# A decode block on one Trainium2 core: the Down loads in two pieces, the end products in two PSUM banks

## The chip, the cores and the metric

The kernel runs on one core of a Trainium2 chip. The metric is the time of one execution in microseconds, as the device reports it. Before the change it was 263.92 us (median of 3 runs, 263.78 to 263.95). Lower is better.

## The reference

One decode step of a transformer block in float32, for 8 sequences with one new token each and a width of 1024: attention over the last 1024 positions of a cache (32 query heads, 4 key and value heads of 128), then a gated MLP with an inner width of 3584. Cut to what matters:

```python
x = A_x                                                   # 8 x 1 x 1024
h = x + attention(layernorm(x))                           # wq, caches, softmax, wo
g = layernorm(h) @ w_gate                                 # 1024 x 3584
u = layernorm(h) @ w_up                                   # 1024 x 3584
h2 = h + (gelu_tanh(g) * u) @ w_down                      # 3584 x 1024: "Down"
```

With only 8 rows of activations the arithmetic is small. What has to be moved is 111 MB of weights and caches.

## The kernel before, in words

All weights and caches come as one stream of loads into two halves of a large SBUF tile `w`, `wbuf[0]` ("a") and `wbuf[1]` ("b"), of 8 MB each. Twelve units of 8 MB fill the two in turn: two for each of wq, K, V, wo, Gate and Up in sets of columns. Every load is issued by SP, in program order, on one queue; a load waits until TensorE has done with the half that it overwrites (`half_a`, `half_b`: marks on TensorE's semaphore).

TensorE runs a loop (L230) over 8 turns. A turn has a product over half b, `half(1, ...)`, then a fold of its four partial sums (L236, `y_sb` and `add2`), then 8 transposes of `source` (L241), then a product over half a, `half(0, ...)`; the turns in `NO_B` and `NO_A` leave one of them out. A product is 8 steps c = 0 to 7, each with 4 matmuls side by side in four column strips of the array (L223); a matmul of 512 columns in float32 gives two records in the trace, so one step has 8 records and one product 64. Waits inside a product come from the list of gates given to `half`: at c = 0 the load's semaphore (`go[0]` or `go[1]`), at later steps `go_later`, where a number of 1 stands for one step of another engine and of 16 for one load. As the loop is the same code for every turn, GpSimd sets `go_later` ahead of time for all turns but the last (L196).

The MLP's last matrix, Down, is 3584 x 1024: 28 chunks of 128 rows, each 0.5 MB. Eight of them (`EARLY`) ride in the units of Gate and Up. The next 16 (`HEAD`) go into `wbuf[0]`, two chunks for each step c, in loads of 10, 4 and 2 chunks (`PARTS`; names `wd0` to `wd2`, tensor `dn`), all released by the end of the product over the unit before. The last four go into `wbuf[1]`: `we0` with two chunks and `we1` with one (`ENDPARTS`, tensor `tails`), and the last chunk in two blocks of columns, `wl0` and `wl1` (`ENDS`, 160 and 96 of each quarter's 256, tensor `ends`).

So the last turn's product over half a (turn 8) starts at c = 0 when `wd0` is there, waits at c = 5 for `wd1` and at c = 7 for `wd2`. VectorE adds its two halves to what was gathered before (`d1`, L423 and L424). Then come the end products (L429), 128 rows against one quarter of 256 columns in each of the four strips: `d1` folded by `add2`, and chunks last - 3, last - 2 and last - 1, all summed in the PSUM bank `acc`. ScalarE copies this sum out (`most`, L444) while the last chunk's two blocks go into two other banks (L455), and VectorE adds each to its columns of `most` (L458). Two stores send the output, `out0` from SP and `out1` from ScalarE's queue.

Of the kernel before, what the change touches and what calls it, by code (L numbers as in the profile page):

```python
# [7 lines left out]
P = 128  # L8
B = 8
D = 1024  # L10
HQ, HKV, DH = 32, 4, 128
REP = HQ // HKV
DF = 3584
EPS = 1e-5
NC = D // P
NQ = 4
QW = D // NQ
# [9 lines left out]
UNITS = 12  # L27
EARLY = 8
HEAD = 16
PARTS = (10, 4, 2)  # L30
ENDPARTS = (2, 1)
ENDS = (160, 96)
AHEAD = 3
PAD = 128


GATE = (1, 16, 16)
TURNS = 9
NO_B = (1, 4)
NO_A = (3,)  # L40
# [2 lines left out]
class Flow:  # L43
# [37 lines left out]
    def run(self, engine, make, *waits, mark=True, gives=None):  # L81
        ins = self.start(engine, make, waits)
        if gives is not None:
            ins.then_inc(*gives)
            return None
        if not mark:
            return None
        self.done[engine] += 1
        ins.then_inc(self.own[engine], 1)
        return self.own[engine], self.done[engine]  # L90

    def move(self, name, out, src, *waits, engine="sync", sem=None):
        s = self.sem(name) if sem is None else sem
        self.start(engine, lambda e: e.dma_start(out, src), waits).then_inc(s, 16)  # L94
        return s, 16


def decode_block(nc, x, units, dn, tails, ends, outs):

    fl = Flow(nc)  # L100
    run, move = fl.run, fl.move
# [3 lines left out]
    def sb(name, *shape):  # L105
        return nc.alloc_sbuf_tensor(name, list(shape), F32).ap()
# [5 lines left out]
    wbuf = [space[:, i * BUF:(i + 1) * BUF] for i in range(2)]  # L112
    sums = [bank(f"sum{i}", 2 * N) for i in range(2)]
    turned = bank("turned", 2 * N)
    acc, fin = bank("acc", N), bank("fin", N)
# [3 lines left out]
    go = [fl.sem("go_a"), fl.sem("go_b")]  # L119
    go_later = [fl.sem(f"go_{i}") for i in range(len(GATE))]  # L120
# [23 lines left out]
    def half_b(k, h=1):  # L144
        return at_mark["b", k, h]
# [5 lines left out]
    for u in range(UNITS):  # L151
        k, i = divmod(u, 2)
# [6 lines left out]
    q0 = EARLY  # L159
    for i, (n, sem) in enumerate(zip(PARTS, (go[0], *go_later[1:]))):  # L160
        c0 = (q0 - EARLY) * D
        move(f"wd{i}", wbuf[0][:, c0:c0 + n * D], dn[i], half_a(passes - 2), sem=sem)
        q0 += n
    assert q0 == EARLY + HEAD
    arrived = {}
    c0 = 0
    for i, n in enumerate(ENDPARTS):
        here = move(f"we{i}", wbuf[1][:, c0:c0 + n * D], tails[i], half_b(nb - 1))
        for r in range(n):
            arrived[q0] = wbuf[1][:, c0 + r * D:c0 + (r + 1) * D], here  # L170
            q0 += 1
        c0 += n * D
    last = q0
    assert last == DF // P - 1
    blocks = []
    a = 0
    for i, (n, src) in enumerate(zip(ENDS, ends)):
        t = wbuf[1][:, c0:c0 + NQ * n]
        blocks.append((a, n, t, move(f"wl{i}", t, src)))
        c0 += NQ * n  # L180
        a += n


    ident = sb("ident", P, P)
# [2 lines left out]
        out=ident, in_=ident, compare_op=ALU.not_equal, fill=1.0, base=0,  # L187
# [4 lines left out]
    add2 = sb("add2", P, 2, 32)  # L192
# [3 lines left out]
    for i, g in enumerate(go_later):  # L196
        run("gpsimd", lambda e: e.memset(note[:, i:i + 1], 0.0), gives=(g, GATE[i] * (passes - 1)))

    own = sb("own", P, HB)
    own_ok = run("vector", lambda e: e.tensor_reduce(  # L200
        out=own, in_=ident.rearrange("p (a b h) -> p b a h", b=HB, h=REP), axis=AX.XY,
# [13 lines left out]
    def half(i, gates):  # L215
        gates = dict(gates)
        for c in range(NC):
            if c in gates:
                take(*gates[c])
            h = c // (NC // 2)  # L220
            for j in range(NQ):
                s = NQ * c + j
                ins = PE.matmul(  # L223
                    sums[i][32 * j:32 * j + 32, h * N:(h + 1) * N], still[i][:, 32 * s:32 * s + 32],
                    wbuf[i][:, s * N:(s + 1) * N],
                    start=(c % (NC // 2) == 0), stop=(c % (NC // 2) == NC // 2 - 1))
            if c % (NC // 2) == NC // 2 - 1:
                mark(ins)

    with PE.Fori(1, TURNS) as i:  # L230
        with PE.If(i != NO_B[0]):
            with PE.If(i != NO_B[1]):
                half(1, [(0, (go[1], 17))])
                take(go_fold, 1)
                for ch in range(2):
                    ins = PE.matmul(turned[0:32, ch * N:(ch + 1) * N], add2[:, ch, :], y_sb,  # L236
                                    start=True, stop=True)
                mark(ins)
        take(go_turn, 1)
        for n in range(NC):  # L240
            ins = PE.transpose(turned[:, n * P:(n + 1) * P], source[:, n * P:(n + 1) * P], ident)  # L241
        mark(ins)
        with PE.If(i != NO_A[0]):
            half(0, [(0, (go[0], 17)), *zip((4, 5, 7), zip(go_later, GATE))])
    fl.done["tensor"] = len(seq)


# [39 lines left out]
    for hf in range(2):  # L287
        done = (half_a, half_b)[hf]
        q_sb = sb(f"q{hf}", P, N)
        tok = run("vector", lambda e: e.tensor_scalar(  # L290
            q_sb, sums[hf][:, 0:N], scale, None, op0=ALU.mult), done(0, 0))
# [23 lines left out]
    for hf in range(2):  # L315
        done = (half_a, half_b)[hf]
        nmax, tot, rtot = (sb(f"{n}{hf}", P, 1) for n in ("nmax", "tot", "rtot"))
        share.append(sb(f"share{hf}", P, HB))
        tok = run("vector", lambda e: e.tensor_reduce(  # L319
            out=nmax, in_=sums[hf], axis=AX.X, op=ALU.max, negate=True), done(1))  # L320
# [5 lines left out]
        tok = run("vector", lambda e: e.reciprocal(rtot, tot), p_ok)  # L326
# [50 lines left out]
    at = sb("at", P, DF // P, 32)  # L377
    gate, ge, up = (sb(n, P, N) for n in ("gate", "ge", "up"))
    down = sb("down", P, D)
    q0 = 0  # L380
    for k, n in enumerate(SETS):
        rows = 32 * n
        tok = run("scalar", lambda e: e.copy(gate[:rows], sums[0][:rows, 0:N]), half_a(4 + k, 0))
        tok = run("vector", lambda e: e.tensor_add(  # L384
            gate[:rows], gate[:rows], sums[0][:rows, N:2 * N]), tok, half_a(4 + k))
        ge_ok = run("scalar", lambda e: e.activation(ge[:rows], gate[:rows], AF.Gelu_apprx_tanh), tok)
        if k == 1:
# [5 lines left out]
        tok = run("scalar", lambda e: e.copy(up[:rows], sums[1][:rows, 0:N]), half_b(4 + k, 0))  # L393
        tok = run("vector", lambda e: e.tensor_add(  # L394
            up[:rows], up[:rows], sums[1][:rows, N:2 * N]), tok, half_b(4 + k))
        run("vector", lambda e: e.tensor_mul(source[:rows, 0:N], up[:rows], ge[:rows]), tok, ge_ok,
            gives=(go_turn, 1))
        t = turned[:, 0:N].rearrange("p (i m) -> p i m", m=P)
# [9 lines left out]
        else:  # L408
# [3 lines left out]
                at_ok, gives=(go_later[0], 1))  # L412
# [3 lines left out]
    tok = run("vector", lambda e: e.tensor_add(  # L416
        down[rows:P], down[rows:P], sums[1][rows:P]), half_b(5), side_ok)
# [4 lines left out]
    d1 = sb("d1", P, N)  # L422
# [1 line left out]
    d1_ok = run("vector", lambda e: e.tensor_add(d1, d1, sums[0][:, N:2 * N]), tok, half_a(6))  # L424


    def quarters(lhs, rhs, *waits, start=False, stop=False):
        for j in range(NQ):
            tok = run("tensor", lambda e: e.matmul(  # L429
                acc[32 * j:32 * j + 32, 0:QW], lhs(j), rhs(j), start=start, stop=stop),  # L430
                *waits, mark=(stop and j == NQ - 1))
        return tok

    def chunk(q, **flags):
        t, here = arrived[q]
        return quarters(lambda j: at[:, q, :], lambda j: t[:, j * QW:(j + 1) * QW], here, at_ok, **flags)

    quarters(lambda j: add2[:, j // 2, :], lambda j: d1[:, (j % 2) * QW:(j % 2) * QW + QW], d1_ok,
             start=True)
    chunk(last - 3)  # L440
    chunk(last - 2)
    tok = chunk(last - 1, stop=True)
    most = sb("most", P, QW)
    most_ok = run("scalar", lambda e: e.copy(most, acc[:, 0:QW]), tok)  # L444


    ahead = sb("ahead", 1, AHEAD)
    for i in range(AHEAD):
        run("vector", lambda e: e.memset(ahead[:, i:i + 1], 0.0), arrived[last - 1][1], d1_ok)

    o_fin = sb("o_fin", P, QW)
    done = []
    for (c0, n, t, here), d_ps in zip(blocks, (fin, sums[1])):
        for j in range(NQ):
            tok = run("tensor", lambda e: e.matmul(  # L455
                d_ps[32 * j:32 * j + 32, 0:n], at[:, last, :], t[:, j * n:(j + 1) * n],
                start=True, stop=True), here, d1_ok, mark=(j == NQ - 1))
        done.append(run("vector", lambda e: e.tensor_add(  # L458
            o_fin[:, c0:c0 + n], most[:, c0:c0 + n], d_ps[:, 0:n]), most_ok, tok))

    for e in both:
        nc.engines[e].br_ne(lap, 0, on_true="never", on_false="through")
    with nc.body("never", valid_engines=both):
        nc.regs_alu(lap, lap, 1, op=ALU.add)
        for e in both:
            nc.engines[e].br_lt(lap, 9, on_true="never", on_false="through").branch_hint(near[e])
    nc.switch_bb("through")

    cut = ENDS[0]
    sent = [move("out0", outs[0], o_fin[:, 0:cut], done[0]),  # L470
            move("out1", outs[1], o_fin[:, cut:QW], done[1], engine="scalar")]


    issued = fl.sem("issued")
# [86 lines left out]
```

## Time and profile before

| What | Value |
|---|---|
| Time, median of 3 runs | 263.92 us |
| Profiled execution: span from its first to its last instruction | 262.3 us |
| TensorE busy (matmuls) | 138.9 us, 53% |
| VectorE, ScalarE, GpSimd busy | 43.8, 13.5, 7.2 us |
| Moved by DMA | 111.31 MB, mean 424 GB/s |
| SP's queue, share of 16 DMA engines over the span | 98.4% |
| Mean granted TensorE clock | 0.805 of full speed |

The profile gives the profiled execution's span but no device time of its own; the median of the runs is 1.6 us above the span. Times inside the trace count from the span's start. "Landing" is the time from a load's issue to its completion. The granted clock is the share of TensorE's full clock that the chip lets through. PE is TensorE, PEld its weight loads, DVE VectorE, ACT ScalarE, POOL GpSimd, SP SyncE; a "q" behind the name is that engine's queue of issues.

### The profile page before, as it was taken

The page shows a single profiled execution, that of the slowest core. Times are in us where ns is not written, and L with a number is a line of the kernel's source. Part 1 is how long each engine was busy: PE and PEld are TensorE (multiplying, and loading weights), DVE is VectorE, ACT ScalarE, POOL GpSimd, SP SyncE. Part 2 cuts the span into 40 slices and gives each one's busy share as a digit, 9 for nine tenths or more (in the row PEclk, how much of TensorE's full clock was granted, in tenths as well). Part 3 has the DMA queues.
Part 4 walks back from the last instruction along what each step waited for, and adds up shares of the span by engine and source line. Part 5 has one row for each costly group of instructions (what it writes and reads, how often), then busy time and mean ns, then how long its engine had stood idle before and what let it go on. Part 6 is the DMA issues. An engine that isn't in the chain of part 4 may idle for free. (4 is left out here: it accounts for less than half of the span.)

```text
span 262.3 us, 2253 instructions
## 1 busy us (share of the span) xinstructions
PE 138.9 (53%) x968; PEld 43.5 (17%) x968; DVE 43.8 (17%) x115; ACT 13.5 (5%) x19; POOL 7.2 (3%) x18
## 2 busy tenths in 40 slices
PE   0025905916706937507908608629409809209985
PEld 0021201301102222102302102122102302002321
DVE  0340100240100140400410101263100300100422
ACT  1000000000030010000000200000300000200000
POOL 5000000100000000100100000000000000000000
PEclk9999965975975986965965957986966968957999
DMA  8998997999899799989979998997999999799895
GB/s 320 485 440 360 480 480 340 460 480 440 360 480 480 320 480 480 440 360 480 480 320 480 480 430 370 480 480 320 480 480 400 400 480 480 320 420 500 370 421 229
DMA packets 3040, 111.31 MB, mean 424 GB/s; under 512 B 472, under 2 KB 728, under 8 KB 992
## 3 DMA queue, kind: packets, MB, share of 16 engines
q1 hardware_dynamic: 2880, 111.23, 98.4%
q10 hardware_dynamic: 160, 0.08, 0.1%
HBM read 111.18 MB, written 0.13 MB: 424 GB/s over the span
## 5 line engine op out<-in xcount | busy, mean ns | idle before, releaser
L223 PE MATMUL sum<-w,still 128*32 128x512 f32 x832 | 115.7, 716 | 98.3 <-PEq L210 98.3
L223 PEld LDWEIGHTS sum<-w,still 128*32 128x32 f32 x832 | 31.9, 129 | 177.7 <-issue 177.7
L241 PE MATMUL turned<-ident,source 128*128 128x128 f32 x64 | 10.1, 310 | 21.1 <-PEq L210 21.1
L241 PEld LDWEIGHTS turned<-ident,source 128*128 128x128 f32 x64 | 8.0, 157 | 26.4 <-issue 26.4
L236 PE MATMUL turned<-y_sb,add 128*32 128x512 f32 x24 | 11.3, 592 | 0.9 <-PEq L210 0.9
L319 DVE TENSOR_REDUCE nmax<-sum 128x1 f32<-128x1024 f32 x2 | 2.4, 1224 | 30.1 <-PE sum L223 30.1
L394 DVE TENSOR_TENSOR up<-up,sum 128x512 f32<-128x512 f32 (+1 forms) x2 | 1.4, 686 | 36.3 <-PE sum L223 36.3
L290 DVE TENSOR_SCALAR q<-sum 128x512 f32<-128x512 f32 x2 | 1.4, 692 | 24.4 <-PE sum L223 24.4
L275 DVE COPY still<-turned 128x1024 f32<-128x1024 f32 x4 | 4.7, 1220 | 4.0 <-PE turned L241 4.0
L384 DVE TENSOR_TENSOR gate<-gate,sum 128x512 f32<-128x512 f32 (+1 forms) x2 | 1.4, 685 | 21.7 <-PE sum L223 21.7
L346 DVE SCALAR_TENSOR_TENSOR o<-sum,share,o 128x128 f32<-128x128 f32 x12 | 4.2, 351 | 4.2 <-PE sum L223 3.8
L343 DVE TENSOR_SCALAR o<-sum,share 128x128 f32<-128x128 f32 x2 | 0.7, 350 | 22.9 <-PE sum L223 22.9
L321 ACT ACT_TABLE_LOAD x1 | 1.3, 1283 | 59.4 <-DVE nmax L319 59.4
L236 PEld LDWEIGHTS turned<-y_sb,add 128*32 128x32 f32 x24 | 2.6, 110 | 8.7 <-issue 8.7
L350 POOL MEMSET still<- 128x1024 f32 x2 | 1.9, 951 | 76.0 <-PE sum L223 76.0
L362 DVE TENSOR_TENSOR y_sb<-y_sb,sum 128x512 f32<-128x512 f32 x1 | 0.7, 686 | 16.0 <-PE sum L223 16.0
L361 ACT COPY y_sb<-sum 128x512 f32<-128x512 f32 x1 | 0.6, 586 | 50.7 <-PE sum L223 50.7
L321 ACT ACTIVATE source<-sum,nmax 128x1024 f32<-128x1024 f32 x2 | 2.2, 1113 | 18.8 <-PE turned L241 18.8
L295 POOL MEMSET still<- 128x1024 f32 x2 | 1.9, 956 | 45.7 <-PE sum L223 45.7
L363 DVE TENSOR_TENSOR y_sb<-y_sb,sum 128x512 f32<-128x512 f32 x1 | 0.7, 689 | 14.1 <-PE sum L223 14.1
L306 DVE COPY still<-turned 128x16 f32<-128x16 f32 x32 | 2.7, 165 | 2.1 <-PE turned L241 2.1
L260 ACT ACT_TABLE_LOAD x2 | 2.6, 1283 | 3.0 <-POOL ident L186 2.9
(61 smaller groups left out, 38.8 us busy)
## 6 DMA issues: line engine op xcount, KB each, us to landing
w<-dn SPq DMA_DIRECT2D x1, 5120.0 KB, 22.9
w<-dn SPq DMA_DIRECT2D x1, 2048.0 KB, 27.4
w<-dn SPq DMA_DIRECT2D x1, 1024.0 KB, 29.4
w<-tails SPq DMA_DIRECT2D x1, 1024.0 KB, 12.8
w<-tails SPq DMA_DIRECT2D x1, 512.0 KB, 13.7
w<-ends SPq DMA_DIRECT2D x1, 320.0 KB, 14.1
w<-units SPq DMA_DIRECT2D x12, 29.5
w<-ends SPq DMA_DIRECT2D x1, 192.0 KB, 14.1
```

Of the source, the lines that this page charges most:

```text
L223: ins = PE.matmul(sums[i][32 * j:32 * j + 32, h * N:(h + 1) * N], still[i][:, 32 * s:32 * s + 32], wbuf[i][:, s * N:(s + 1) * N], start=(c ...
L236: ins = PE.matmul(turned[0:32, ch * N:(ch + 1) * N], add2[:, ch, :], y_sb, start=True, stop=True)
L241: ins = PE.transpose(turned[:, n * P:(n + 1) * P], source[:, n * P:(n + 1) * P], ident)
L260: tok = run("scalar", lambda e: e.activation(sd, ve, AF.Sqrt), tok)
L275: run("vector", lambda e: e.tensor_copy(still[i].rearrange("p (c j m) -> p c j m", c=NC, j=NQ), turned.rearrange("p (c m) -> p c m", c=NC) ...
L290: tok = run("vector", lambda e: e.tensor_scalar(q_sb, sums[hf][:, 0:N], scale, None, op0=ALU.mult), done(0, 0))
L295: cleared.append(run("gpsimd", lambda e: e.memset(still[hf], 0.0), done(0)))
L306: run("vector", lambda e: e.tensor_copy(to[:, :, b, s, a, REP * b:REP * b + REP].rearrange("p k (h i) -> p k h i", h=2), frm[:, s, a * HB ...
L319: tok = run("vector", lambda e: e.tensor_reduce(out=nmax, in_=sums[hf], axis=AX.X, op=ALU.max, negate=True), done(1))
L321: p_ok = run("scalar", lambda e: e.activation(source, sums[hf], AF.Exp, bias=nmax, accum_out=tot), tok, at_mark["t", 1 + hf])
L346: tok = run("vector", lambda e: e.scalar_tensor_tensor(out, o3[:, b], share[hf][:, b:b + 1], o_sb, op0=ALU.mult, op1=ALU.add), tok, done(2 ...
L350: cleared[hf] = run("gpsimd", lambda e: e.memset(still[hf], 0.0), done(2))
```

## The change

- The 16 chunks of `wbuf[0]` come in loads of 12 and 4 instead of 10, 4 and 2. The gates inside the product follow: c = 0 for the 12, c = 6 for the 4 (`GATES`). One semaphore less is used.
- The last four chunks come from one tensor `ends` in four loads: two chunks, one chunk, and the last chunk as 192 and 64 columns of each quarter (`EDGE` and `REST`).
- The end products are cut at column 192: each quarter's first 192 columns are summed in `acc` (`edge`), its last 64 in `fin` (`rest_ps`), through all five terms, the last chunk included.
- The copy `most` and the two additions go. ScalarE copies `edge` and VectorE `rest_ps` into `o_fin`. The stores are cut at 192 instead of 160.

```diff
-PARTS = (10, 4, 2)
-ENDPARTS = (2, 1)
-ENDS = (160, 96)
+PARTS = (12, 4)
+EDGE = 192
+REST = QW - EDGE
+ENDS = (2 * D, D, NQ * EDGE, NQ * REST)
...
-GATE = (1, 16, 16)
+GATE = (1, 16)
+GATES = (4, PARTS[0] // 2)
...
-            half(0, [(0, (go[0], 17)), *zip((4, 5, 7), zip(go_later, GATE))])
+            half(0, [(0, (go[0], 17)), *zip(GATES, zip(go_later, GATE))])
...
+    edge, rest_ps = acc[:, 0:EDGE], fin[:, 0:REST]
-    def quarters(lhs, rhs, *waits, start=False, stop=False):
-        for j in range(NQ):
-            tok = run("tensor", lambda e: e.matmul(
-                acc[32 * j:32 * j + 32, 0:QW], lhs(j), rhs(j), start=start, stop=stop),
-                *waits, mark=(stop and j == NQ - 1))
+    def quarters(lhs, rhs, *waits, sides=((edge, 0), (rest_ps, EDGE)), start=False, stop=False):
+        for out, a in sides:
+            for j in range(NQ):
+                tok = run("tensor", lambda e: e.matmul(
+                    out[32 * j:32 * j + 32], lhs(j), rhs(j, a, out.shape[1]), start=start, stop=stop),
+                    *waits, mark=(stop and j == NQ - 1))
...
-    tok = chunk(last - 1, stop=True)
-    most = sb("most", P, QW)
-    most_ok = run("scalar", lambda e: e.copy(most, acc[:, 0:QW]), tok)
+    chunk(last - 1, here[1], 2 * D, QW)
+    c0 = 3 * D
+    edge_ok = chunk(last, here[2], c0, EDGE, sides=((edge, 0),), stop=True)
+    rest_ok = chunk(last, here[3], c0 + NQ * EDGE, REST, sides=((rest_ps, 0),), stop=True)
...
-        done.append(run("vector", lambda e: e.tensor_add(
-            o_fin[:, c0:c0 + n], most[:, c0:c0 + n], d_ps[:, 0:n]), most_ok, tok))
+    done = [
+        run("scalar", lambda e: e.copy(o_fin[:, 0:EDGE], edge), edge_ok),
+        run("vector", lambda e: e.tensor_copy(o_fin[:, EDGE:QW], rest_ps), rest_ok),
+    ]
```

TensorE's product over half a, with its waits (`go_a` is the first load, `go_0` a step of VectorE, `go_1` and `go_2` the later loads), before:

```order
L223 MATMUL sum<-w,still 32x512 [waits go_a_done]
L223 MATMUL sum<-w,still 32x512 x15
L223 MATMUL sum<-w,still 32x512 [waits go_0_done]
L223 MATMUL sum<-w,still 32x512 x3
L223 MATMUL sum<-w,still 32x512 [waits go_1_done]
L223 MATMUL sum<-w,still 32x512 x7
L223 MATMUL sum<-w,still 32x512 [waits go_2_done]
L223 MATMUL sum<-w,still 32x512 x3
```

and after, with the line numbers of the changed kernel:

```order
L215 MATMUL sum<-w,still 32x512 [waits go_a_done]
L215 MATMUL sum<-w,still 32x512 x15
L215 MATMUL sum<-w,still 32x512 [waits go_0_done]
L215 MATMUL sum<-w,still 32x512 x7
L215 MATMUL sum<-w,still 32x512 [waits go_1_done]
L215 MATMUL sum<-w,still 32x512 x7
```

The wait for the second load has moved from the 21st matmul to the 25th, and the one for a third load is gone; the first wait is for 12 chunks.

TensorE's end products, behind the loop's closing branch, before:

```order
L230 COMPARE_AND_BRANCH
L429 MATMUL acc<-d,add 32x256 x4
L429 MATMUL acc<-w,at 32x256 x12
L455 MATMUL fin<-w,at 32x160 x4
L455 MATMUL sum<-w,at 32x96 x4
```

and after:

```order
L424 MATMUL acc<-d,add 32x192 x4
L424 MATMUL fin<-d,add 32x64 x4
L424 MATMUL acc<-w,at 32x192 x4
L424 MATMUL fin<-w,at 32x64 x4
L424 MATMUL acc<-w,at 32x192 x4
L424 MATMUL fin<-w,at 32x64 x4
L424 MATMUL acc<-w,at 32x192 x4
L424 MATMUL fin<-w,at 32x64 x4
L424 MATMUL acc<-w,at 32x192 x4
L424 MATMUL fin<-w,at 32x64 x4
```

Every group of four matmuls of 256 columns is now one of 192 and one of 64 in another bank, 40 matmuls in place of 24, and the last chunk's share goes into the same two sums.

More of the change, by code (lines that the diff above doesn't have):

```diff
@@ L95, in move, with decode_block @@
         return s, 16
-def decode_block(nc, x, units, dn, tails, ends, outs):
+def decode_block(nc, x, units, dn, ends, outs):
     fl = Flow(nc)
@@ L164, in decode_block @@
     assert q0 == EARLY + HEAD
-    arrived = {}
+    last = DF // P - 1
+    assert P * sum(ENDS) == P * D * (last + 1 - q0)
+    here = []
     c0 = 0
[L167 to L176, printed above, removed]
     for i, (n, src) in enumerate(zip(ENDS, ends)):
[L178 to L181, printed above, removed]
+        here.append(move(f"we{i}", wbuf[1][:, c0:c0 + n], src, half_b(nb - 1)))
+        c0 += n
     ident = sb("ident", P, P)
@@ L424, in decode_block @@
     d1_ok = run("vector", lambda e: e.tensor_add(d1, d1, sums[0][:, N:2 * N]), tok, half_a(6))
-    def quarters(lhs, rhs, *waits, start=False, stop=False):
-        for j in range(NQ):
-            tok = run("tensor", lambda e: e.matmul(
-                acc[32 * j:32 * j + 32, 0:QW], lhs(j), rhs(j), start=start, stop=stop),
-                *waits, mark=(stop and j == NQ - 1))
-        return tok
-    def chunk(q, **flags):
-        t, here = arrived[q]
-        return quarters(lambda j: at[:, q, :], lambda j: t[:, j * QW:(j + 1) * QW], here, at_ok, **flags)
@@ L438, in decode_block @@
[L438 to L441, printed above, removed]
-    tok = chunk(last - 1, stop=True)
-    most = sb("most", P, QW)
-    most_ok = run("scalar", lambda e: e.copy(most, acc[:, 0:QW]), tok)
+    edge, rest_ps = acc[:, 0:EDGE], fin[:, 0:REST]
[5 more added lines that the diff above has]
+                    *waits, mark=(stop and j == NQ - 1))
+        return tok
@@ new lines, in chunk @@
+    def chunk(q, ready, c0, w, **flags):
+        return quarters(
+            lambda j: at[:, q, :],
+            lambda j, a, n: wbuf[1][:, c0 + w * j + a:c0 + w * j + a + n], ready, at_ok, **flags)
+    quarters(lambda j: add2[:, j // 2, :],
+             lambda j, a, n: d1[:, (j % 2) * QW + a:(j % 2) * QW + a + n], d1_ok, start=True)
+    chunk(last - 3, here[0], 0, QW)
+    chunk(last - 2, here[0], D, QW)
+    chunk(last - 1, here[1], 2 * D, QW)
+    c0 = 3 * D
+    edge_ok = chunk(last, here[2], c0, EDGE, sides=((edge, 0),), stop=True)
@@ L447, in decode_block @@
+    rest_ok = chunk(last, here[3], c0 + NQ * EDGE, REST, sides=((rest_ps, 0),), stop=True)
     ahead = sb("ahead", 1, AHEAD)
     for i in range(AHEAD):
-        run("vector", lambda e: e.memset(ahead[:, i:i + 1], 0.0), arrived[last - 1][1], d1_ok)
+        run("vector", lambda e: e.memset(ahead[:, i:i + 1], 0.0), here[1], d1_ok)
     o_fin = sb("o_fin", P, QW)
[L452 to L458, printed above, removed]
-            o_fin[:, c0:c0 + n], most[:, c0:c0 + n], d_ps[:, 0:n]), most_ok, tok))
+    done = [
+        run("scalar", lambda e: e.copy(o_fin[:, 0:EDGE], edge), edge_ok),
+        run("vector", lambda e: e.tensor_copy(o_fin[:, EDGE:QW], rest_ps), rest_ok),
+    ]
@@ L467, in decode_block @@
     nc.switch_bb("through")
-    cut = ENDS[0]
-    sent = [move("out0", outs[0], o_fin[:, 0:cut], done[0]),
-            move("out1", outs[1], o_fin[:, cut:QW], done[1], engine="scalar")]
+    sent = [move("out0", outs[0], o_fin[:, 0:EDGE], done[0]),
+            move("out1", outs[1], o_fin[:, EDGE:QW], done[1], engine="scalar")]
     issued = fl.sem("issued")
@@ L525 @@
     dn = np.concatenate([by_row(a, n) for a, n in zip(at, PARTS)])
-    at = [EARLY + HEAD + sum(ENDPARTS[:i]) for i in range(len(ENDPARTS))]
-    tails = np.concatenate([by_row(a, n) for a, n in zip(at, ENDPARTS)])
-    cuts = [sum(ENDS[:i]) for i in range(len(ENDS) + 1)]
-    by_group = rows[-1].reshape(P, NQ, QW)
-    ends = np.concatenate([by_group[:, :, a:b].reshape(-1) for a, b in zip(cuts, cuts[1:])])
+    grouped = rows[-1].reshape(P, NQ, QW)
+    ends = np.concatenate([a.reshape(-1) for a in (
+        by_row(len(rows) - 4, 2), rows[-2], grouped[..., 0:EDGE], grouped[..., EDGE:])])
     arrays = {
-        "x": own(A_x).reshape(B, D), "units": own(units), "dn": dn, "tails": tails, "ends": ends,
+        "x": own(A_x).reshape(B, D), "units": own(units), "dn": dn, "ends": ends,
     }
@@ L541 @@
     out = nc.dram_tensor("out", (P * QW,), F32, kind="ExternalOutput").ap()
-    cut = P * ENDS[0]
+    cut = P * EDGE
     outs = [o.rearrange("(p n) -> p n", p=P) for o in (out[0:cut], out[cut:P * QW])]
-    aps["ends"] = [
-        aps["ends"][P * NQ * a:P * NQ * b].rearrange("(p n) -> p n", p=P)
-        for a, b in zip(cuts, cuts[1:])
-    ]
-    for name, parts in (("dn", PARTS), ("tails", ENDPARTS)):
+    for name, parts in (("dn", [n * D for n in PARTS]), ("ends", ENDS)):
         flat, f0 = aps[name], 0
@@ L551 @@
         for n in parts:
-            aps[name].append(flat[f0:f0 + P * n * D].rearrange("(p n) -> p n", p=P))
-            f0 += P * n * D
+            aps[name].append(flat[f0:f0 + P * n].rearrange("(p n) -> p n", p=P))
+            f0 += P * n
     decode_block(nc, outs=outs, **aps)
```

## The prediction

> **What bounds the kernel now.** I read the page first, then the chain of waits, then the timeline of the last 17 us, and last a table of windows for TensorE's granted clock. The page's span and DMA rows, the last DMA row of the chain, and the issues with their time to landing:
>
> ```profile
> span 262.3 us, 2253 instructions
> q1 hardware_dynamic: 2880, 111.23, 98.4%
> ...
> 245.45 14.08 DMA w<-ends
> ...
> w<-dn SPq DMA_DIRECT2D x1, 5120.0 KB, 22.9
> ...
> out<-o_fin ACTq DMA_DIRECT2D x1, 48.0 KB, 1.6
> ```
>
> SP's queue keeps the sixteen DMA engines busy for 98.4% of the span, and the chain ends with a load (L94, the block `wl0`) that lands at 259.53. The loads are the bound, and TensorE waits for them. What matters is how TensorE follows the last loads:
>
> ```profile
> 224.68 1.28 SPq L94 DMA_DIRECT2D w<-dn  x3
> ...
> 246.16 1.09 PE L241 MATMUL turned<-ident,source 128*128 128x128 f32 x8
> ...
> 247.67 4.50 PE L223 MATMUL sum<-w,still 128*32 128x512 f32 x40 [0.41 <-PEq L210]
> ...
> 252.57 1.92 PE L223 MATMUL sum<-w,still 128*32 128x512 f32 x16 [0.40 <-PEq L210]
> ...
> 255.05 1.06 PE L223 MATMUL sum<-w,still 128*32 128x512 f32 x8 [0.56 <-PEq L210]
> 256.18 0.69 DVE L424 TENSOR_TENSOR d<-d,sum 128x512 f32<-128x512 f32 x1 [4.12 <-PE sum L223]
> ...
> 256.92 0.64 PE L429 MATMUL acc<-d,add 128*32 128x256 f32 x8 [0.80 <-DVE d L424]
> ...
> 257.45 1.07 PE L429 MATMUL acc<-w,at 128*32 128x256 f32 x16
> ...
> 258.74 0.64 PE L429 MATMUL acc<-w,at 128*32 128x256 f32 x8 [0.21 <-DMA w<-tails]
> ...
> 259.44 0.37 ACT L444 COPY most<-acc 128x256 f32<-128x256 f32 x1 [17.69 <-PE acc L429]
> ...
> 259.57 0.48 PE L455 MATMUL fin<-w,at 128*32 128x160 f32 x8 [0.20 <-DMA w<-ends]
> ...
> 260.03 0.37 PE L455 MATMUL sum<-w,at 128*32 128x96 f32 x8
> 260.12 0.32 DVE L458 TENSOR_TENSOR o_fin<-most,fin 128x160 f32<-128x160 f32 x1 [1.19 <-PE fin L455]
> 260.47 0.25 DVE L458 TENSOR_TENSOR o_fin<-most,sum 128x96 f32<-128x96 f32 x1
> 260.47 0.35 SPq L94 DMA_DIRECT2D out<-o_fin  x1
> 260.75 0.35 ACTq L94 DMA_DIRECT2D out<-o_fin  x1
> ```
>
> The first Down load (10 chunks, issued at 224.68, 22.9 us to landing) lands at 247.58, 0.33 us after the transposes end (246.16 + 1.09 = 247.25), and the main product starts at 247.67. It waits again at 252.57 for the 4 chunks and at 255.05 for the 2. Those three waits are harmless: TensorE works in the landing order and is through with its part 1.1 us after the last of them. After 256.92 it waits for `tails` and `ends` alike, so TensorE is never more than a few tenths behind the loads.
>
> **The change part by part.**
>
> *Loads.* The bytes are the same; three Down issues become two, on the same queue with the same release. Between the starts at 247.67 and 255.05, 6 chunks came in 7.38 us, 1.23 us each, 2.46 for two. The 12-chunk load so lands at 247.58 + 2.46 = 250.04, and its product can start at 250.13 instead of 247.67. The other 4 chunks are there by 255.05 as before. The last four chunks' worth comes from 255.05 to 260.03, 4.98 us or 1.25 each, in four issues; at 1.23 it would be 4.92. So the two issues more that this stretch has cost 0.06, and the one that is saved is worth 0.03 on the loads; I take 0 of it for the end, which the loads no longer set, and keep 0 to -0.1.
>
> *Main product, at full clock.* 40 records take 4.50 us and 16 take 1.92: (4.50 - 1.92) / 24 = 0.1075 us per record, and 0.20 at the end. All 64 records now follow on one another, since the 4 chunks are there before c = 6 begins (250.13 + 48 x 0.1075 = 255.29 against 255.05): end at 250.13 + 64 x 0.1075 + 0.20 = 257.21, against 255.05 + 1.06 = 256.11 before. The slack that the smaller pieces gave is used up, 1.10 us of it.
>
> *End products.* VectorE's addition L424 and its two hand-overs take 256.92 - 256.11 = 0.81, so the products begin at 258.02. A group of 256 columns costs 1.07 - 0.64 = 0.43 (16 records less 8), and 0.21 at the end. Each is now 192 and 64 columns, eight instructions in place of four. The nearest rows are 160 columns (0.48) and 96 (0.37): 0.0017 us per column, which leads from 256 (0.64) straight to 96, with no floor; so 192 + 64 costs what 256 does, and I take that. Upper end: a 64-column group costs as much as the 96-column one, 0.16 instead of 0.11, over five groups +0.25 us. `d1` and the three chunks before the last: 4 x 0.43, to 259.74; their loads landed by 258.74. The last chunk's two blocks land as the stream ends, the 64-column one at about 260.0, and TensorE starts it at 259.74 + 0.32 = 260.06, so neither makes it wait: end at 259.74 + 0.43 + 0.21 = 260.38, against 260.40 before.
>
> *Out of PSUM.* `most`, ScalarE's copy, goes away; it hid behind the wait for `ends`. In its place ScalarE copies 192 columns at the very end and VectorE 64. The additions of 160 and 96 columns took 0.32 and 0.25, so 64 columns take some 0.22, begun 0.07 after TensorE: 260.67, 0.05 before the old 260.72. ScalarE's 192 columns are below the 0.37 of 256; TensorE is through with them 0.11 earlier, so it ends by 260.38 - 0.11 + 0.06 + 0.33 = 260.66. Both output issues leave at about 260.70 (the later of the old ones at 260.75), and a landing takes 1.6 as before. ScalarE's own output issue stands behind its copy, which is done at that moment. Sum at full clock: -0.05 us, up to +0.2 with the floor. Nothing is gained, and TensorE is now the last link of the chain, with no slack from 250.13 on.
>
> **The clock.** TensorE now stands idle from 247.25 to 250.13, 2.88 us in place of 0.42. What that does, a table of windows of 3.413 us shows, with one row of the timeline ahead of it; cut at these points no row from the first recorded change (34.66) on has a clock between 0.50 and 1.00, so the clock changes only there. Columns: window, length, TensorE busy (records), other engines, granted clock, DMA.
>
> ```profile
> 42.03 8.47 PE L223 MATMUL sum<-w,still 128*32 128x512 f32 x64 [9.74 <-PEq L210]
> ...
> 31.25:34.66 3.41, 1.05 (x12) 0.13 (x4) 0.69 (x1) 0.00 (x0) 0.96 (x1) 1.00 1.42 614
> 34.66:38.07 3.41, 0.00 (x0) 0.00 (x0) 0.00 (x0) 0.00 (x0) 0.00 (x0) 0.50 0.71 307
> ...
> 41.48:44.90 3.41, 2.86 (x16) 0.92 (x20) 0.00 (x0) 0.00 (x0) 0.00 (x0) 0.50 0.84 365
> 44.90:48.31 3.41, 3.41 (x36) 1.08 (x32) 0.69 (x1) 0.00 (x0) 0.00 (x0) 1.00 0.75 326
> ...
> 51.72:55.14 3.41, 1.50 (x10) 0.86 (x8) 1.81 (x23) 0.00 (x0) 0.00 (x0) 1.00 0.71 307
> 55.14:58.55 3.41, 0.00 (x0) 0.00 (x0) 0.88 (x11) 0.00 (x0) 0.00 (x0) 0.50 1.42 614
> ...
> 68.79:72.20 3.41, 1.62 (x16) 0.27 (x8) 1.22 (x1) 0.42 (x1) 0.00 (x0) 1.00 0.71 307
> 72.20:75.62 3.41, 0.00 (x0) 0.00 (x0) 0.39 (x2) 2.07 (x3) 0.00 (x0) 1.00 1.42 614
> ...
> 79.03:82.44 3.41, 1.71 (x9) 0.49 (x13) 0.00 (x0) 0.00 (x0) 0.00 (x0) 0.50 1.20 518
> 82.44:85.86 3.41, 3.41 (x21) 0.90 (x17) 0.00 (x0) 0.00 (x0) 0.00 (x0) 0.50 0.93 403
> ...
> 92.68:96.10 3.41, 1.42 (x12) 0.97 (x10) 1.72 (x4) 1.21 (x2) 0.00 (x0) 1.00 0.71 307
> 96.10:99.51 3.41, 0.00 (x0) 0.00 (x0) 1.12 (x1) 0.00 (x0) 0.00 (x0) 0.50 1.38 595
> ...
> 167.78:171.19 3.41, 1.58 (x4) 0.22 (x2) 1.76 (x2) 0.00 (x0) 0.00 (x0) 1.00 0.71 307
> 171.19:174.60 3.41, 0.28 (x3) 0.31 (x4) 2.51 (x9) 0.20 (x1) 0.00 (x0) 1.00 1.42 614
> ...
> 246.28:249.70 3.41, 3.00 (x28) 1.54 (x32) 2.30 (x4) 0.00 (x0) 0.00 (x0) 1.00 0.90 384
> 249.70:253.11 3.41, 3.01 (x32) 0.93 (x28) 1.44 (x3) 0.00 (x0) 0.00 (x0) 1.00 0.97 413
> ```
>
> After a window at 1.00 with 1.05, 1.42 or 1.50 us of work the next has 0.50; after one with 1.58 or 1.62 it stays at 1.00. So some 1.54 us of work in a window keep the clock. Back from 0.50 it comes after 2.86 us and not after 1.71. The 64 records from 42.03 on took 8.47 instead of the 7.08 that 64 take at full clock (64 x 0.1075 + 0.20); they ran at 0.50 until 44.90, 2.87 us, of which 1.39 were lost, half. In the traced execution the window 246.28 to 249.70 had 3.00 us. With the change it has the transposes alone, 247.25 - 246.28 = 0.97, below every window that kept its clock: the clock falls at 249.70, the product starts at half pace, the window to 253.11 is busy for 2.98, and the clock returns there. Of 2.98 us at half pace half is lost: +1.49 on a chain that has no slack. Sum: -0.05 + 1.49 = +1.44.
>
> Where the windows lie against the program another execution may show differently; nothing in one trace ties them to it. For a fall, the idle part of a window must be over 3.41 - 1.54 = 1.87: it begins between 247.25 + 1.87 - 3.41 = 245.71 and 250.13 - 1.87 = 248.26, which is 2.55 of 3.41, 75% of all positions. In 0.45 of all positions the whole cold stretch falls on work and costs 3.41 / 2 = 1.71; in 0.30, where the clock falls before 250.13 (at 249.12 the earliest), it costs 1.20 to 1.71.
>
> [...]
>
> **How it stands to the median.** The profiled span is 262.3, the median of the runs 263.92, 1.6 us around it that this change leaves alone. I put the shift on the median: 265.36.
>
> **The rivals.**
> 1. *The clock holds* (not slower): the window's edge lies so that no window loses 1.87 us to the gap, 25% of the positions. Then 263.92 - 0.05 = 263.87, up to 264.1 with the floor of narrow products. For it: the gap is shorter than a window. Against: it leaves as little as 3.41 - 2.88 = 0.53 us of work in one, and 1.50 was too little. The point that decides is 1.54 us of work.
> 2. *Only an idle time longer than a window counts*: the work in it doesn't matter, the clock holds at every position, and the time is the same 263.9. For it: no row here has a gap as short as this one with a whole product behind it. Against: the windows at 31.25 and 51.72. [...]
> 3. *Two cold windows*: the clock falls early, before the product starts, and the next window has too little work to bring it back (the bound lies between 1.71 and 2.86 us). A fall at 249.12 leaves 2.40 us in the next, in the open part. Then it is cold until 249.12 + 6.83 = 255.95, and half of 5.82 is lost: 263.9 + 2.9 = 266.8. Only the earliest positions can do it.
> 4. *The end gains*: with one load fewer, an addition less and 64 columns behind the last load instead of 96, the end would be shorter if the product weren't late. The rows give 0.03 for the load and 0.05 for the last copy; with what ScalarE takes over, 263.8, still within a measurement's error. Against: TensorE has no slack left.
>
> **How the numbers follow.** One cold window 0.68, two 0.06, clock held by position 0.16 (somewhat under the 25%, since the traced position may be the usual one), held by the second rival 0.05, the fourth 0.05, of which 0.03 for a gain that no row shows. In one cold window the sum is 265.36 at the traced position and 265.6 where all of it falls on work; I take 265.4, with a range of its own of 265.0 to 265.9 (1.20 to 1.71, and up to 0.25 of floor). To hold 8 in 10 the range must take in the held clock: 263.7 to 266.0, which leaves out the two cold windows. A measurement of this kernel tells 0.2%, 0.53 us, from no change: slower 0.74, within it 0.23, faster 0.03.
>
> **What would show it.** Right: in the profile after, the main product's first records start at about 250.1 with a granted clock of 0.50, 64 of them without a wait and an end near 258.7; the chain of waits ends in TensorE rows and in the copies, no longer in a load; the output issues leave at about 262.2. Wrong: full clock at 250.1 and an end at 257.2 (rivals 1 and 2, told apart by the work in the window before); 0.50 until about 256 (rival 3); a wait for `ends` left in the last groups, which would say that the loads still bound the end; groups of 64 columns at above 0.16 us.

## The result, and the profile after

| | before | changed |
|---|---|---|
| Time, median | 263.87 us (263.78 to 263.95, 4 runs) | 266.86 us (266.78 to 267.84, 4 runs) |
| Span of the profiled execution | 262.3 us | 265.5 us |
| Ratio | | 1.0123 (95% interval 1.0108 to 1.0138) |

The change made the kernel slower by 2.99 us; the forecast was 1.5. In the profile after, the page's first and DMA rows and the chain, and below them the end of the timeline:

```profile
span 265.5 us, 2306 instructions
...
q1 hardware_dynamic: 2736, 111.25, 97.2%
q10 hardware_dynamic: 160, 0.07, 0.1%
q8 instruction: 1, 0.02, 0.0%
...
251.31 8.80 PE sum L215 x64
260.14 0.70 DVE d L416
...
263.34 0.23 DVE o_fin L451
```

```profile
247.96 1.09 PE L233 MATMUL turned<-ident,source 128*128 128x128 f32 x8
...
251.31 8.77 PE L215 MATMUL sum<-w,still 128*32 128x512 f32 x64 [2.26 <-PEq L202]
...
260.88 0.53 PE L424 MATMUL acc<-d,add 128*32 128x192 f32 x8 [0.80 <-DVE d L416]
...
262.98 0.29 PE L424 MATMUL fin<-w,at 128*32 128x64 f32 x8
263.23 0.32 ACT L450 COPY o_fin<-acc 128x192 f32<-128x192 f32 x1 [19.68 <-PE acc L424]
263.34 0.23 DVE L451 COPY o_fin<-fin 128x64 f32<-128x64 f32 x1 [2.38 <-PE fin L424]
263.57 0.35 SPq L96 DMA_DIRECT2D out<-o_fin  x1
263.60 0.36 ACTq L96 DMA_DIRECT2D out<-o_fin  x1
```

The chain no longer holds a load: it is the Down product, the addition L416 and the end products, as forecast. The product starts at 251.31 (forecast 250.13) and takes 8.77 (forecast 8.57 with one cold window, 7.08 with none). What follows it, 0.80 us for the addition and its hand-overs and 2.39 for the end products, fits the forecast of 0.81 and 2.36 to 0.03. The windows, with the columns as in the prediction, show the fall of the clock:

```profile
248.64:252.06 3.41, 1.15 (x12) 0.51 (x14) 2.84 (x5) 0.00 (x0) 0.00 (x0) 1.00 0.91 389
252.06:255.47 3.41, 3.41 (x20) 1.08 (x16) 0.22 (x1) 0.00 (x0) 0.00 (x0) 0.50 1.00 422
255.47:258.88 3.41, 3.41 (x36) 1.26 (x32) 0.69 (x1) 0.00 (x0) 0.00 (x0) 1.00 0.98 394
```

1.15 us of work in one window, then one window at 0.50, all of it on the product. But the loads are late too. TensorE's starts on the first two units are shown here, of before and then of after; the last line is the row of a DMA queue, from 28 to 31 us after:

```profile
22.69 9.60 PE L223 MATMUL sum<-w,still 128*32 128x512 f32 x64 [6.51 <-PEq L210]
42.03 8.47 PE L223 MATMUL sum<-w,still 128*32 128x512 f32 x64 [9.74 <-PEq L210]
```

```profile
22.72 9.06 PE L215 MATMUL sum<-w,still 128*32 128x512 f32 x64 [6.66 <-PEq L202]
43.28 9.02 PE L215 MATMUL sum<-w,still 128*32 128x512 f32 x64 [11.50 <-PEq L202]
...
q8 instruction: 1, 0.02, 2.0%
```

Unit 1 is there at the same moment, unit 2 is 1.25 us late, and the loads keep that delay (the last unit before Down is used from 236.78 on, before from 235.55). Between the two stands a queue that the old trace does not have: one packet of instructions, 16 KB, at 29.2 us, which takes 0.96 us. The third difference is at the end. The last store is issued at 263.60 and the span ends at 265.49, 1.89 us later; before it was 260.75 and 262.34, 1.59.

### The profile page after: what moved, and what is told of

Read it like the earlier page. It is cut to its first block, busy times and chain, and to the rows that moved or that the text cites. A ratio compares the mean times of both kernels' runs of the same rounds, so it can differ in the third digit from the quotient of the medians.

```text
span 265.5 us, 2306 instructions
## 1 busy us (share of the span) xinstructions
PE 140.8 (53%) x1000; PEld 46.0 (17%) x1000; DVE 43.4 (16%) x114; ACT 13.5 (5%) x19; POOL 7.2 (3%) x17
## 5 line engine op out<-in xcount | busy, mean ns | idle before, releaser
L215 PE MATMUL sum<-w,still 128*32 128x512 f32 x832 | 117.1, 726 | 99.9 <-PEq L202 99.9
L215 PEld LDWEIGHTS sum<-w,still 128*32 128x32 f32 x832 | 32.6, 130 | 180.2 <-issue 180.2
L233 PE MATMUL turned<-ident,source 128*128 128x128 f32 x64 | 11.2, 333 | 21.0 <-PEq L202 20.9
L233 PEld LDWEIGHTS turned<-ident,source 128*128 128x128 f32 x64 | 9.0, 171 | 26.3 <-issue 26.3
## 6 DMA issues: line engine op xcount, KB each, us to landing
w<-dn SPq DMA_DIRECT2D x1, 2048.0 KB, 29.2
```

The costliest lines, as they stand in the source:

```text
L215: ins = PE.matmul(sums[i][32 * j:32 * j + 32, h * N:(h + 1) * N], still[i][:, 32 * s:32 * s + 32], wbuf[i][:, s * N:(s + 1) * N], start=(c ...
```

## The experiments

Theory A: TensorE's longer program (16 more matmuls, 64 more instructions) brings a fetch of code into the load stream, and the late first Down load costs the clock. Theory B: the loads, as they are now cut, move the stream. The kernel before, run beside these on the same chips, had medians of 263.77 to 263.85.

**Loads alone.** `loads_12_4`: the kernel before with

```diff
-PARTS = (10, 4, 2)
+PARTS = (12, 4)
-GATE = (1, 16, 16)
+GATE = (1, 16)
-            half(0, [(0, (go[0], 17)), *zip((4, 5, 7), zip(go_later, GATE))])
+            half(0, [(0, (go[0], 17)), *zip((4, 6), zip(go_later, GATE))])
```

> The kernel before with the loads and gates of the change alone (12 and 4 chunks); its end products, copies and stores are the old ones, and TensorE's program is no longer than before. Theory A (the change lost time in two places: TensorE's longer program brings a fetch of instructions into the load stream, which moves every later load by 1.2 us; and the late first Down load lets TensorE's clock fall): no fetch here, the product over the second unit starts at 42.0 us as before, the Down product at 250.1 us, and its 64 records take 8.3 to 8.8 us where a window goes cold and 7.1 where none does; time 265.2 to 265.8 in the cold executions, 264.1 in the others. Theory B (the loads themselves move the stream): second unit at 43.3 us, a time near 266.8.

Measured: 265.72 us, ratio 1.0070 (1.0047 to 1.0094). The six executions lie in three groups: 264.23; 265.59, 265.68 and 265.76; 266.85 and 266.91. The profiled one is of the last group, and its timeline and windows show why:

```profile
42.11 9.89 PE L223 MATMUL sum<-w,still 128*32 128x512 f32 x64 [10.01 <-PEq L210]
...
250.16 9.97 PE L223 MATMUL sum<-w,still 128*32 128x512 f32 x64 [3.11 <-PEq L210]
```

```profile
245.81:249.22 3.41, 1.24 (x9) 0.86 (x8) 2.06 (x3) 0.00 (x0) 0.00 (x0) 1.00 0.68 293
249.22:252.64 3.41, 2.48 (x12) 0.69 (x16) 0.99 (x3) 0.00 (x0) 0.00 (x0) 0.50 1.00 427
252.64:256.05 3.41, 3.41 (x20) 0.92 (x16) 0.00 (x0) 0.00 (x0) 0.00 (x0) 0.50 0.96 403
256.05:259.46 3.41, 3.41 (x36) 1.08 (x32) 0.69 (x1) 0.00 (x0) 0.00 (x0) 1.00 0.93 365
```

No fetch, unit 2 in time, the product at 250.16 as forecast for the change. The window with 1.24 us of work lost the clock, the next one with 2.48 did not bring it back, and the product took 9.97 instead of 7.08: rival 3 of the prediction, in this execution. Theory B falls. The loads cost 1.9 us in the median; that this is the clock and nothing else, `loads_rows128` shows below.

**Ends alone.** `ends_only`: the changed kernel with `PARTS = (10, 4, 2)`, `GATE = (1, 16, 16)` and gates at 4, 5 and 7.

> The changed kernel with the old Down loads (10, 4 and 2 chunks): the end products in two banks, the copies and the stores are the new ones. Theory A: TensorE's program is as long as in the changed kernel, so one fetch on its own queue at about 29 us, the second unit's product at 43.3 instead of 42.0 and every load 1.2 us later; the clock holds (product in the landing order, as before); time 265.0 to 265.3. Theory B: no loss, 263.8 to 264.0, since the old loads are back.

Measured: 265.26 us (264.98 to 265.73), ratio 1.0055 (1.0042 to 1.0068). The fetch is back, unit 2 starts at 43.48, and the Down product follows the loads at full clock. The new ends alone cost 1.45 us, though in them TensorE waits 0.33 us for a load of the last chunk, so that it isn't TensorE that is late.

**The change with a program of the old length.** `after_short`: the changed kernel without `chunk(last - 3, ...)` and `chunk(last - 2, ...)`, whose share of the output is missing.

> The changed kernel without the end products of two chunks (the fourth and third from the end; their share is missing in the output), which brings TensorE's program back to the length that it had before; loads, banks, copies and stores are those of the change. Theory A: no fetch, second unit at 42.0 us, Down product at 250.1 us, a cold window in most executions; against the changed kernel 1.2 us less for the fetch and 0.86 us less for the products left out: 264.7 with a full cold window, 263.6 or somewhat less with the clock held. Theory B: only the 0.86 us less, 265.9.

Measured: 264.71 us (264.11 to 265.90), ratio 1.0044 (1.0027 to 1.0062), 2.15 us less than the changed kernel, of which 0.86 are the products left out. No instruction queue in the trace; unit 2 and Down at:

```profile
42.05 8.82 PE L215 MATMUL sum<-w,still 128*32 128x512 f32 x64 [9.39 <-PEq L202]
...
250.06 8.77 PE L215 MATMUL sum<-w,still 128*32 128x512 f32 x64 [2.46 <-PEq L202]
```

**Code alone.** `code_16` and `code_8`: the kernel before with 16 or 8 matmuls more behind the last end product.

```diff
+    for i in range(16):
+        j = i % NQ
+        run("tensor", lambda e: e.matmul(
+            turned[32 * j:32 * j + 32, 0:64], at[:, last, :], t[:, 0:64], start=True, stop=True), mark=False)
```

> The kernel before with 16 more matmuls of 64 columns at the very end of TensorE's program, into a bank that nobody reads any more: the program is as long as the changed kernel's, and nothing else is different. Theory A: one fetch at about 29 us, the second unit's product at 43.3 us, all landings 1.2 us later, 265.1 us. Theory B: 263.9 us, no fetch.

> The kernel before with 8 more matmuls of 64 columns at the end of TensorE's program, 32 instructions in place of 64. Theory A says that a boundary lies between the old length and 64 instructions more; this halves the interval: a fetch on a queue of its own and the second unit's product at 43.2 us or later if it lies in the lower half, 42.0 us and no fetch if in the upper one.

Measured: 265.00 us (264.74 to 265.17) with 16, ratio 1.0047 (1.0034 to 1.0060); 263.75 with 8, in one execution, without a fetch and with unit 2 at 42.06. With 16:

```profile
q8 instruction: 1, 0.02, 2.0%
```

```profile
22.76 8.81 PE L223 MATMUL sum<-w,still 128*32 128x512 f32 x64 [6.72 <-PEq L210]
43.16 8.85 PE L223 MATMUL sum<-w,still 128*32 128x512 f32 x64 [11.59 <-PEq L210]
```

These matmuls run at 261.3 us, behind everything; what they cost, 1.2 us, is paid at 31 us, where the packet of instructions moves, 230 us before they run. They don't hold up the end themselves: the last unit before Down is used 1.12 us later than before, and the span is 1.08 us longer. With 32 instructions more than the old length there is no fetch, with 64 there is one: a boundary lies between. The fetch isn't hidden here, where the loads keep the sixteen DMA engines busy for 98.4% of the span before.

**The clock held.** `loads_warm` and `after_warm`: the loads alone, and the change, with work for TensorE in the gap, behind the transposes.

```diff
         mark(ins)
+        for n in range(2):
+            PE.matmul(fin[0:32, 0:N], ident[0:32, 0:32], x_sb[0:32, 0:N], start=True, stop=True)
```

> The loads of 12 and 4 chunks on the kernel before, and two more matmuls behind the transposes of every turn (32 rows of x_sb, 512 columns, into the bank fin, which the end products start afresh): they give TensorE some 1.7 us of work in the gap before the Down product, so that 1.2 us of it stay idle, less than the 1.87 that a window can lose. Theory A (the clock): no execution goes cold, the 64 records of the Down product take 7.1 us from 250.1 on, and all executions lie at 264.0 to 264.2. Theory C (the product is slow because it reads while the loads write, or for another reason that lies in the 12-chunk load): 265.6 to 266.9, as without these matmuls.

> The changed kernel with the same two matmuls behind the transposes. Theory A: the fetch stays (TensorE's program is even longer), the Down product starts at about 251.3 and takes 7.1 us instead of 8.8; 265.0 to 265.3 in all executions, 1.6 to 1.7 us less than the changed kernel. Theory C: 266.8 as without them.

Measured: 263.99 us (263.78 to 266.41, 12 runs), ratio 1.0032 (1.0011 to 1.0053), and 265.16 (264.97 to 266.75, 6 runs), ratio 1.0051 (1.0038 to 1.0064). Both medians are where theory A puts them, but 5 of 12 and 1 of 6 executions went cold all the same by their times, at 265.6 to 266.8, the profiled ones among them. Of `loads_warm`:

```profile
248.12 1.90 PE L244 MATMUL fin<-x_sb,ident 32*32 32x512 f32 x4
250.74 8.77 PE L223 MATMUL sum<-w,still 128*32 128x512 f32 x64 [0.73 <-PEq L210]
```

```profile
247.49:250.90 3.41, 2.68 (x15) 0.99 (x17) 2.58 (x4) 0.00 (x0) 0.00 (x0) 1.00 0.99 422
250.90:254.31 3.41, 3.41 (x20) 1.08 (x16) 0.48 (x2) 0.00 (x0) 0.00 (x0) 0.50 0.97 410
```

A window with 2.68 us of work lost the clock, more than any limit so far. Most of that work has 32 rows of the array in use ("32*32"), where the other forms have 128. So I put up theory A2, that a window counts work by the rows in use, and tried the same gap with as much work of 128 rows, eight matmuls of 128 columns:

```diff
+        for n in range(8):
+            PE.matmul(fin[0:32, 0:P], ident[:, 0:32], ident, start=True, stop=True)
```

> The loads of 12 and 4 chunks on the kernel before, and eight more matmuls behind the transposes of every turn: 128 columns and all 128 rows (ident against ident, into the bank fin), 1.7 us of streaming as in loads_warm, whose matmuls had 32 rows. Theory A2 (a window counts streamed time in proportion to the array's rows in use, so that the 32-row matmuls counted a quarter): the clock holds in every execution, the Down product takes 7.1 us from 250.1 on, all times 263.9 to 264.2. Rival (extra matmuls only shift chances, or only weights that read new data count): a third of the executions cold again, 265.6 to 266.4.

Measured: 263.94 us (263.81 to 264.53, 11 runs), ratio 1.0009 (1.0000 to 1.0018). None of 11 went cold by their times, and the profiled execution has the forecast of the held clock (250.13, 7.08, 258.02) to 0.03 us:

```profile
247.83 1.93 PE L244 MATMUL fin<-ident 128*32 128x128 f32 x16
250.16 7.07 PE L223 MATMUL sum<-w,still 128*32 128x512 f32 x64 [0.40 <-PEq L210]
258.04 0.64 PE L431 MATMUL acc<-d,add 128*32 128x256 f32 x8 [0.80 <-DVE d L426]
```

The added matmuls differ from those of `loads_warm` in their number too, 8 in place of 2. But the window at 167.78 in the prediction's table held the clock with 1.58 us in 4 records, all of the fold ("128*32"), and a window of `loads_warm` with 1.95 us, of which 1.90 are its 4 records of 32 rows, lost it:

```profile
209.94:213.35 3.41, 1.95 (x6) 0.34 (x4) 1.18 (x3) 0.00 (x0) 0.00 (x0) 1.00 1.33 576
213.35:216.76 3.41, 0.00 (x0) 0.00 (x0) 0.00 (x0) 0.00 (x0) 0.00 (x0) 0.50 0.80 346
```

So it is the rows in use, not the number of matmuls. Three of the eleven, at 264.4 to 264.5, are half a microsecond above the rest; their traces were not taken, and I can't say why.

**The stores.** Four kernels on the one before: `blocks_192_64` has `ENDS = (192, 64)`; `stores_192_64` and `stores_128_128` keep the blocks and cut the stores at 192 or 128, both waiting for `done[1]`; `store_one` sends all 256 columns from SP behind `done[1]`.

> The kernel before with the last chunk's blocks, and so the stores, cut at 192 columns instead of 160; everything else, the copy of the sum ahead of them included, is old. The second store has rows of 256 bytes instead of 384, but is issued 0.2 us or more after the first. In the changed kernel the two stores are issued 0.03 us apart and the last one took 1.9 us instead of 1.6. If narrow rows are slow, 1.9 here too and 264.1 us; if two stores at one time get in each other's way, 1.6 to 1.7 here and 263.8 us.

> The kernel before with its two stores cut at column 192 and both issued when the last addition is done, as close together as in the changed kernel; all else is old. If it is the two stores at one time, or their narrow rows, that took the changed kernel's last store 1.9 us: 1.9 here from issue to the span's end, 264.0 to 264.2 us. If not, 1.6 and 263.8 us.

> The same with the cut at column 128: two stores at one time with rows of 512 bytes each. If narrow rows are what costs, 1.6 us and 263.8; if it is two stores at one time, 1.9 and 264.1.

> The kernel before with one store of all 256 columns, rows of 1024 bytes, issued by SP when the last addition is done. If either narrow rows or two stores at one time cost, it has neither: 1.6 us or less after the issue, 263.7 to 263.8 us, or a little less than before, since the old last issue stood on another queue.

The issues and their times to landing, of `stores_192_64` and of `stores_128_128`:

```profile
260.66 0.35 SPq L94 DMA_DIRECT2D out<-o_fin  x1
260.67 0.38 ACTq L94 DMA_DIRECT2D out<-o_fin  x1
...
out<-o_fin SPq DMA_DIRECT2D x1, 96.0 KB, 1.7
out<-o_fin ACTq DMA_DIRECT2D x1, 32.0 KB, 1.9
```

```profile
261.06 0.35 SPq L94 DMA_DIRECT2D out<-o_fin  x1
261.07 0.38 ACTq L94 DMA_DIRECT2D out<-o_fin  x1
...
out<-o_fin SPq DMA_DIRECT2D x1, 64.0 KB, 1.7
out<-o_fin ACTq DMA_DIRECT2D x1, 64.0 KB, 1.8
```

From the last issue to the span's end it takes 1.90 us with both stores at one time and rows of 256 bytes, 1.85 with rows of 512 bytes, 1.73 with the stores 0.14 apart (`blocks_192_64`, rows of 256 bytes), 1.75 with one store of everything, 1.59 in the old kernel with 0.28 between them. The rows' width accounts for 0.05 at most. The less apart the two issues, the longer the last one takes, and the other traces fit: 1.63 to 1.64 with 0.17 between them (`loads_12_4`, `loads_warm`, `loads_rows128`). But `store_one` has no second store and yet not the 1.6 that was expected of it, so whether it is the company or the amount of data still to be written is not shown. In the times it is at the limit of what can be told: 264.05 us, ratio 1.0009 (1.0000 to 1.0018); 264.12, 1.0012 (1.0003 to 1.0021); `store_one` 263.96, 1.0006 (0.9997 to 1.0015); `blocks_192_64` 264.17, 1.0014 (1.0005 to 1.0023). `blocks_192_64`, whose stores are apart, is no faster than those that send them together, so the times don't bear out the traces here. None of the kernels tried beats the one before.

## Why the prediction was wrong

- **Direction and the mechanism that was forecast: right, but 1.2 us of the loss came from elsewhere.** TensorE became the last link, the clock fell in the gap that the 12-chunk load opens, and `loads_rows128` shows the same loads without loss once the clock is held. Start 250.13, product 7.08 and end products at 258.02 are what that trace has, to 0.03.
- **The step that failed: the loads, "its product can start at 250.13".** It started at 251.31, 1.18 us late. The end products were counted by their time on TensorE ("192 + 64 costs what 256 does", which held: 2.39 us for 2.36), and not as code. The 16 matmuls more are 64 instructions, past a boundary (no fetch with 32 more, in `code_8`) behind which a block of 16 KB is fetched, in the middle of a load stream that fills the DMA engines for 98.4% of the span before. `code_16` has this alone, +1.2 us, and `after_short` shows the changed kernel's loads in time without it.
- **The clock's term: mis-sized by 0.20.** All of the cold window fell on work: 8.77 - 7.08 = 1.69, where the traced position of before gave 1.49. The bounds (1.20 to 1.71) hold it.
- **The chance of two cold windows, 0.06, was too low.** I let the window's position be free, which one trace could not show and the traces since bear out (the first edge behind the span's start lies between 0.05 us, in `loads_12_4`, and 2.88, in the changed kernel), and kept the transposes' end at 247.25. But the product before them runs at half pace until the clock returns, so their end moves with the window: 247.05 in `loads_12_4`, 248.19 in `loads_warm`, both by the rows. Of the 17 executions with the new loads and no added work (the changed kernel, `loads_12_4`, `after_short`), 15 were cold by their times; 264.23 of `loads_12_4` and 264.11 of `after_short` lie too near to what the loads alone allow to tell. Five lie some 1.0 to 1.2 us above the rest of their kind, as far as a second cold window would put them: 266.85 and 266.91 of `loads_12_4`, 265.8 and 265.9 of `after_short`, and 267.84 of the changed kernel. Only the one at 266.91 has a trace, and it shows the two windows.
- **"A landing takes 1.6 as before": mis-sized by 0.30.** The new copies end together, and the stores leave 0.03 us apart instead of 0.28; the section on the stores says how far that is shown to be the cause.
- **The sum.** Measured against the sum for one cold window, 265.36: +1.18 for the fetch, +0.20 for the clock, +0.30 for the stores, +0.03 in the chain, and -0.26 because the profiled execution has 1.32 us around its span (266.81 to 265.49) where I had taken 1.58 (263.92 to 262.34): 266.81, the time of the profiled execution; the median is 266.86. In all profiled executions with a time of their own it is 1.31 to 1.39, so the 1.58 set the span of one execution against the median of others. That rival 3 named 266.8 is chance; the profiled execution had one cold window.
- **Rival 2, that only an idle time longer than a window counts, is out:** an idle time of 2.26 us (251.31 less 249.05) was enough. Rival 4 had nothing to gain from: in `loads_12_4` the last load lands at 260.0, as before.
- **Left open:** whether 267.84 had a second cold window, why one packet of 16 KB holds the stream up by 1.1 to 1.9 us (1.12 in `code_16`, 1.23 in the changed kernel, 1.87 in `ends_only`, at the last unit), and at which instruction the boundary lies.

## What to carry to other kernels

Where loads fill the DMA engines from end to end (98.4% of the span here), a few dozen more instructions may not be free even behind the last deadline (here 32 were, 64 cost 1.2 us): look in the profile for an instruction queue that was not there, and count code before splitting matmuls. When a load is made bigger, ask not only when its data arrive but how little TensorE has to do in any 3.4 us until then: here it lost half its clock in a gap of 2.26 us (the changed kernel), in 15 of the 17 executions with these loads by their times, and eight matmuls over all 128 rows in the gap held it in 11 of 11, at 0.1 us in the median. Last stores that leave at one moment took up to 0.3 us longer in the traces; in the times that is too little to tell.

## What the runs showed of the hardware

Eleven traces, all but those of the three kernels whose stores alone were changed, were cut into windows of 3.413 us from one edge each; from the first recorded change on no window that lies within the span has a clock between 0.50 and 1.00. A window need not be idle to lose the clock, and the limit lies near the 1.54 us of the prediction. In these traces, of the windows that hold main products and folds alone, all 128 rows of the array in use, the clock fell after up to 1.39 us of work and stayed from 1.44 on, both in `blocks_192_64`:

```profile
168.16:171.57 3.41, 1.39 (x4) 0.16 (x2) 1.95 (x3) 0.00 (x0) 0.00 (x0) 1.00 0.71 307
171.57:174.99 3.41, 0.47 (x3) 0.50 (x4) 2.32 (x8) 0.20 (x1) 0.00 (x0) 0.50 1.42 614
...
69.17:72.59 3.41, 1.44 (x16) 0.24 (x8) 1.23 (x1) 0.60 (x1) 0.00 (x0) 1.00 0.75 326
72.59:76.00 3.41, 0.00 (x0) 0.00 (x0) 0.39 (x2) 1.89 (x3) 0.00 (x0) 1.00 1.37 595
```

The first holds the fold, which works in one strip of 32 columns, the second a product, which works in four: the columns in use make no difference that the rows show. The array's rows in use do. Two windows of `loads_warm` hold 1.90 us of 32-row matmuls and otherwise transposes: the clock fell with 2.81 us in all (52.92) and stayed with 2.89 (93.88). An estimate from these two and the limits found here, with the transposes taken in full: 32 of 128 rows count for a fifth to a third of their time. One window of end products alone, over all 128 rows, lost the clock with 1.74 us (`ends_only`, 259.96); why, no run shows.

Back from 0.50 the clock came after windows with 2.73 us of products and more (`loads_warm`, 80.23), and not after 2.57 and less (`ends_only`, 61.98); in `loads_warm` a window that was busy throughout, with 32-row matmuls and transposes (175.80), did not bring it back either.

Transposes count too: a window of `loads_12_4` with transposes alone, 1.57 us by the rows, kept the clock. Whether in full is open: two windows with transposes and the end of a fold lost it, with 1.56 us (`ends_only`, 92.70) and 1.57 (`code_8`, 90.79), where 1.44 us of products had held it.

```profile
92.21:95.63 3.42, 1.57 (x14) 1.26 (x12) 1.62 (x3) 1.21 (x2) 0.00 (x0) 1.00 0.84 364
95.63:99.04 3.41, 0.14 (x2) 0.00 (x0) 1.23 (x1) 0.00 (x0) 0.00 (x0) 1.00 0.71 308
```
